# Chunks of alpha, k and q loaded in runs of one token, and the turned k sent by ScalarE's queue two slots apart

## The chip, the core and the metric

The kernel runs on one core of a Trainium2 chip. A core has TensorE (matmuls; the profile writes PE, and PEld for its weight loads), VectorE (DVE), ScalarE (ACT), GpSimd (POOL) and SyncE (SP), and 16 DMA engines. [...] The metric is the device time of one execution, in microseconds (us).

## What is computed

A gated linear recurrence over 768 tokens (batch 4, 8 heads, head dimension D = 48) feeds a two-layer network with a SiLU, over all 3072 tokens:

```python
def _attn_ref(q, k, v, alpha):
    state = np.zeros((B, H, D, D))
    for t in range(S):
        state = alpha[:, :, t, :, None] * state + np.einsum('bhd,bhe->bhde', k[:, :, t], v[:, :, t])
        y[:, :, t] = np.einsum('bhd,bhde->bhe', q[:, :, t], state)

def _moe_ref(x, w_in, w_out):          # x: 3072 x 384, d_ff: 2048
    h = x @ w_in
    g = h * (1.0 / (1.0 + np.exp(-h)))
    return g @ w_out
```

## The kernel before

**The recurrence.** The 768 tokens of a batch row are cut into 6 chunks of C = 128, so there are NT = 24 chunks n = 0..23, chunk index `ci = n // 4`, batch row `b = n % 4`. A chunk is worked in stages. `products(n)` brings alpha, then k, into the layout [two heads x 64 partitions, tokens], scans alpha (`u`, L734) and multiplies k by it into `kp`. `quotient(n)` does the same for q (scan L764, product L770). `scores(n)` multiplies kp and qp on TensorE; ScalarE copies the result out of PSUM (L818, L821) and GpSimd masks it (L825). `values(n)` multiplies by v, and `states(n)` adds k-transposed times v to the state of the batch row. For `states`, k is needed with tokens on the partitions, as tile `kn`.

**Early and late chunks.** Chunks 0..7 (`n < NA`, NA = 8) are transposed on TensorE. From chunk 8 on (the "late" chunks; 16 of them) three tiles `late["quads"]` hold alpha, k and q (`at`, `kt`, `qt` in the profile), one buffer each. VectorE transposes them in blocks of 32 x 32 by `turned` (L708), three times per chunk: `al<-at`, `turn<-kt`, `turn<-qt`. Right after each, `load(n + 1, name)` fills the tile for the next chunk. A DMA of `load` (L486) writes 32 partitions, 4 heads, 4 neighbouring tokens of 48 floats in one run (768 bytes). Four of them make one tile: each half of the heads is written twice, the second time 32 columns further left, so that the upper 32 partitions hold elements 32 to 47 in the columns where the lower hold 0 to 31. As partition b holds tokens 4b to 4b+3, the transpose has to write with a step of four elements to put the tokens in order.

**k for `states`.** `flip(n)` (late chunks with `ci < 5`, that is n = 8..19) transposes `kp` on VectorE (L780) into the one buffer `turn`, and SyncE at once writes that tile to a DRAM scratch `flips` (L782, 256 KB). In the next step `land(n)` reads it back with the blocks rearranged, in four DMAs of 64 KB (L790), into `kn`. The tile `turn` has one buffer, used in turn by the transposed k, the transposed q and the flip.

**The order.** The loop over steps (STEPS = 25) has four slots per step; after each slot `fill` emits pieces of the network's matmuls that have come due. For the late steps, with a lag of 1 for the stages that work on the chunk of the step before:

```python
stages = [[(land, 1), (scores, 1)], [(products, 0)], [(quotient, 0)],
          [(values, 1), (states, 1), (flip, 0)]]
```

TensorE's instructions are kept in the order in which this loop writes them. On the other engines the framework's scheduler may move an instruction past others, by its own estimates, except where `tc.keep_in_program_order` forbids it; what it decides is then fixed in the program. The loads of SyncE stand in one queue; each of its DMAs signals one of eight semaphores in rotation, and waits until the transfer that used the same semaphore before it has landed.

**The network.** Groups of 512 tokens go through `enter` (w_in) and `leave` (w_out), with block products in the manner of Strassen and Winograd. `enter` cycles through three PSUM banks `ps_m`: a product goes into a bank, ScalarE copies it out (L950), VectorE adds it to what is there (L958), and SiLU runs on ScalarE (L955; L923 in the plain form of the first groups, L863 is the copy of `values` into `xt`). `leave` uses two banks `ps_o` (copies L1054, L1073, L1078 on ScalarE, sums L1047 and L1056 on VectorE). `audit` reads the weights and alpha again to check their range (L681, L683, L697); its last tiles go through the quads once the chunks are done.

Of the kernel before, what the change touches and what calls it, by code (L numbers as in the profile page):

```python
# [8 lines left out]
F32 = mybir.dt.float32  # L9
I32 = mybir.dt.int32  # L10
# [345 lines left out]
def quotients(  # L356
# [19 lines left out]
    nc = tc.nc  # L376
    dve, act, gps = nc.vector, nc.scalar, nc.gpsimd

    late = {}
# [14 lines left out]
    B, H, S, D = q.shape  # L394
    C = 128
    NCH = S // C
    NP = H // 2
    HD = H * D
# [3 lines left out]
    NT = B * NCH  # L402
# [9 lines left out]
    def pool(name, bufs=1, space=None):  # L412
        kw = {} if space is None else {"space": space}
        return ctx.enter_context(tc.tile_pool(name=name, bufs=bufs, **kw))
# [10 lines left out]
    dram = pool("dram", 2, bass.MemoryType.DRAM)  # L425
# [29 lines left out]
    NA = 2 * GB  # L455
# [8 lines left out]
    ctxs = {}  # L464

    def load(n, names="akq"):
        if n == NT:
            return
        c = ctxs.setdefault(n, dict(zip(("ci", "b"), divmod(n, B))))
        b, rows = c["b"], slice(c["ci"] * C, c["ci"] * C + C)  # L470
        for name, src in (("a", alpha), ("k", k), ("q", q)):
            if name not in names:
                continue
            x = src[b, :, rows, :]
            if n < NA:
                c[name] = nat[name][n % NIN]
                nc.sync.dma_start(c[name][:, :, 0:D], x.transpose([1, 0, 2]))
                continue

            c[name] = late["quads"][name]
            for u in range(2):
                for i in range(2):
                    r = 64 * u + 32 * i
                    nc.sync.dma_start(  # L486
                        c[name][r : r + 32, 32 * (1 - i) :][:, 0 : 4 * NP * D].rearrange(
                            "p (g c) -> p g c", g=NP),
                        x[u::2].rearrange("h (b j) d -> b h (j d)", j=4))

    NV = 2
    vns = [fix.tile([128, H, 64], F32, name=f"vn{i}") for i in range(NV)]
# [3 lines left out]
    def load_v(n):  # L496
        c = ctxs.setdefault(n, dict(zip(("ci", "b"), divmod(n, B))))
        x = v[c["b"], :, c["ci"] * C : c["ci"] * C + C, :].transpose([1, 0, 2])
        t = c["v"] = vns[n % NV]
        if n < NA:  # L500
            nc.sync.dma_start(t[:, :, 0:D], x)
            return
        nc.sync.dma_start(t[:, 0 : H // 2, 0:D], x[:, 0 : H // 2])
        for e in range(2):
            nc.sync.dma_start(t[CH * e : CH * e + CH, H // 2 :, 0:D], x[CH - CH * e : C - CH * e, H // 2 :])
# [7 lines left out]
    def fetch():  # L513

        if wide and sources:
# [4 lines left out]
            coming.append(bits)  # L520

    load(0)
    load(1)
    for i in range(4):
        fetch()
# [47 lines left out]
    quads = w_in.rearrange("p k (q i c) -> p i k q c", i=4, c=128)  # L573
# [83 lines left out]
    def audit():  # L657


        flat = alpha.rearrange("b h s d -> (b h s d)").rearrange("(p c) -> p c", p=128)  # L660
        assert 2 * HD <= 32 + 4 * NP * D
        todo = [(flat[:, c : c + AW], AW, 0) for c in range(0, flat.shape[1], AW)]
        if wide:
            todo += [(moe_w_in[t * 128 : t * 128 + 128, c : c + 512], 512, 1)
                     for c in range(0, DF, 512) for t in range(NKT)]
            todo += [(moe_w_out[f * 128 : f * 128 + 128, :], HD, 1) for f in range(NFT)]
        alone = sum(2 * x[1] > 32 + 4 * NP * D or x[2] == 0 for x in todo)
        for kind in (0, 1):
            n = sum(x[2] == kind for x in todo)
            if n:  # L670
                seen.append([fix.tile([128, n], F32, name=f"seen{kind}{i}") for i in range(2)])
        at = [0, 0]
        landed = []

        def begin(src, n, kind):
            at = len(landed)
            t = late["look"].tile([128, 512, 2], I32, name="bits").rearrange("p n w -> p (n w)") if (
                at < alone) else late["quads"]["akq"[at % 3]].bitcast(I32)
            if kind == 0:
                landed.append(t[:, 0:n].bitcast(F32))  # L680
                nc.sync.dma_start(landed[-1], src)  # L681
            else:
                nc.sync.dma_start(t[:, 0 : 2 * n], src.bitcast(I32))  # L683
                landed.append(t[:, 0 : 2 * n].rearrange("p (n w) -> p n w", w=2)[:, :, 1])

        for i, (src, n, kind) in enumerate(todo):

            while len(landed) < min(i + (1 if i + 1 < alone else 3), len(todo)):
                begin(*todo[len(landed)])
            x = landed[i]  # L690
            yield
            i = at[kind]
            at[kind] += 1
            for which, op in ((0, ALU.max), (1, ALU.min)):
                if kind == 1 or which == 0:
                    tc.keep_in_program_order(
                        dve.tensor_reduce(seen[kind][which][:, i : i + 1], x, axis=AX, op=op,  # L697
                                          apply_absolute_value=True))
# [5 lines left out]
        return t[:, 1 : NP * W + 1].rearrange("p (j c) -> p j c", c=W)[:, :, 0:C]  # L704

    def turned(x, to):
        x = x[:, 32:].rearrange("p (g j d) -> p g j d", j=4, d=D)
        dve.transpose(to.rearrange("p g (b j) -> p g j b", j=4), x[:, :, :, 0:32])  # L708

    def products(n):  # L710

# [28 lines left out]
        if n >= NA:  # L740
            ps["k"] = late["turn"].tile([128, NP, C], F32, name="turn")
            turned(c["k"], ps["k"])
            load(n + 1, "k")
# [28 lines left out]
    def flip(n):  # L772

        c = ctxs[n]
        if n < NA or c["ci"] == NCH - 1:
            return
        t = late["turn"].tile([128, NP, C], F32, name="turn").rearrange("p c (j d) -> p c j d", j=NP)
        dve.transpose(t, c["kp"].rearrange("p j (c i) -> p c j i", i=32))  # L780
        c["flip"] = dram.tile([128, NP * C], F32, name="flips")
        nc.sync.dma_start(c["flip"], t.rearrange("p c j d -> p (c j d)"))  # L782

    def land(n):
        c = ctxs[n]
        if "flip" in c:
            c["kn"] = work.tile([128, NP, C], F32, name="kn")
            x = c.pop("flip").rearrange("(r d) (i x) -> i d r x", r=4, i=4)
            for i in range(4):
                nc.sync.dma_start(c["kn"][32 * i : 32 * i + 32], x[i])  # L790

    def scores(n):
        c = ctxs[n]
# [364 lines left out]
    def go_on():  # L1158
# [3 lines left out]
        done += 1  # L1162

    audits = audit()
    done, bridged = 0, 0
    STEPS = NT + 1
# [4 lines left out]
    def settle():  # L1171

        first.close()
        late.update(look=pool("look"), part=pool("part"), turn=pool("turn"),
                    xc=pool("xc").tile([128, len(SUMS_X), TB], F32, name="xc"),
                    wx=pool("wx").tile([128, 8, NQ, 128], F32, name="wx"))
        quads = pool("quads")
        late["p"] = pool("p").tile([128, NP * W + 1], F32, name="p")
        late["quads"] = {name: quads.tile([128, 32 + 4 * NP * D], F32, name=f"{name}t") for name in "akq"}
        for name, t in late["quads"].items():  # L1180
            gps.memset(t, 1.0 if name == "a" else 0.0)
        load(NA)
# [20 lines left out]
    for step in range(STEPS):  # L1203
        if step == 1:
            load(NIN)
        stages = [[(scores, 1)], [(products, 0)], [(values, 1)], [(states, 1)]]
        if step == 1:

            stages = stages[1::-1] + stages[2:]
        elif step >= NA:  # L1210
            stages = [[(land, 1), (scores, 1)], [(products, 0)], [(quotient, 0)],
                      [(values, 1), (states, 1), (flip, 0)]]
        for slot, group in enumerate(stages):
            for stage, lag in group:
                n = step - lag
                if not 0 <= n < NT:
                    continue
                stage(n)
                if stage is values:
                    bridged = n + 1  # L1220
                if stage is states and n + 1 + NIN < NA:
                    load(n + 1 + NIN)
                if stage is states and n + NV < NT:
                    load_v(n + NV)
            if step * SLOTS + slot == (NA + 1) * SLOTS - 1:
                x = decayed.rearrange("p (o i c) -> p o i c", o=2, c=C)
                for r, o in later:
                    gps.memset(x[r, o, :, 0:CH], 0.0)
            fill(step, slot)
            if step * SLOTS + slot >= NA * SLOTS - 1 and conv_done[1] == NFT and not late:  # L1230
                settle()
# [82 lines left out]
```

## Time and profile before

| what | us |
|---|---|
| median of 3 runs (556.2 to 557.51) | 556.21 |
| the profiled execution | 557.26 |
| its span, first to last instruction | 555.5 |
| TensorE busy in the span | 541.4 |
| VectorE busy | 445.4 |
| ScalarE busy | 208.5 |
| GpSimd busy | 76.1 |

The profile comes from one execution, 557.26 us long. Its span is 1.76 us shorter, and the median of the three runs lies 1.05 us below it. The granted TensorE clock was 0.999 of full speed. The page gives for each engine the busy time, for each group of instructions the mean duration and what ended the idle time before them, and for each group of DMAs the median from issue to landing. A line that begins with SPq is an instruction of SyncE's queue, with the time it took to issue. The view of waits lists for each engine whose work it waited for, with total, number and longest. The timeline lists instructions by start time; neighbours of one group are merged, with their number after the x. A float32 matmul is two records in the trace.

### The profile page before, as it was taken

What the parts mean: (1) busy time and instruction counts of PE and PEld (TensorE: products, weight loads), DVE (VectorE), ACT (ScalarE), POOL (GpSimd) and SP (SyncE); (2) the same over time, 40 slices, a digit from 0 to 9 for tenths busy, and PEclk for the clock granted to TensorE, in tenths of its full rate; (3) what the DMA queues carried; (4) which work ended last, traced back from release to release, by engine and by line L of the source; (5) the groups of instructions that cost most, each with busy time, mean ns of one, the idle gap of its engine ahead of it and who ended that gap; (6) DMA issues with size and microseconds to landing.
All of it is one profiled execution on the core that took longest, in us unless ns stands there. A gap on an engine that the chain in (4) does not pass through costs nothing. (4 is left out here: it accounts for less than half of the span.)

```text
span 555.5 us, 12640 instructions
## 1 busy us (share of the span) xinstructions
PE 541.4 (97%) x5026; PEld 489.7 (88%) x5026; DVE 445.4 (80%) x801; ACT 208.5 (38%) x466; POOL 76.1 (14%) x146
## 2 busy tenths in 40 slices
PE   6999999999999999999999999999999999999996
PEld 4788887998899999899999999988998999999996
DVE  5897788974999899997998986998884796945431
ACT  2556653223333253353353353344263342332100
POOL 3210000222210212021011021021121000001000
PEclk9999999999999999999999999999999999999999
DMA  9998971164454625355545654617642135500000
GB/s 215 246 249 210 232 195 33 47 161 116 117 136 125 159 63 138 86 145 149 139 112 139 193 139 120 191 27 183 170 137 91 54 91 169 172 11 22 10 24 30
DMA packets 99217, 70.09 MB, mean 126 GB/s; under 512 B 56272, under 2 KB 88656, under 8 KB 99152
## 3 DMA queue, kind: packets, MB, share of 16 engines
q1 hardware_dynamic: 97232, 65.30, 45.1%
q0 software_dynamic: 1920, 3.93, 2.0%
q8 instruction: 40, 0.66, 0.5%
q14 instruction: 25, 0.20, 0.1%
HBM read 61.34 MB, written 7.86 MB: 125 GB/s over the span
## 5 line engine op out<-in xcount | busy, mean ns | idle before, releaser
L388 PE MATMUL ps_o<-w_out,g 128*128 128x192 f32 x768 | 134.0, 328 | 0.5 <-DVE o L1056 0.5
L388 PEld LDWEIGHTS ps_o<-w_out,g 128*128 128x128 f32 x768 | 125.6, 190 | 3.5 <-DVE o L1056 1.0
L388 PE MATMUL ps_m<-xt,w_in 128*128 128x256 f32 x480 | 113.6, 383 | 1.5 <-ACT xt L863 1.1
L388 PEld LDWEIGHTS ps_m<-xt,w_in 128*128 128x128 f32 x480 | 89.1, 190 | 14.4 <-ACT xt L863 1.6
L388 PE MATMUL ps_o<-wt,g 128*128 128x192 f32 x576 | 99.7, 326 | 0.0
L388 PEld LDWEIGHTS ps_o<-wt,g 128*128 128x128 f32 x576 | 95.1, 190 | 1.6 <-issue 0.2
L388 PE MATMUL ps_m<-xc,w_in 128*128 128x256 f32 x288 | 70.7, 382 | 0.0
L388 PEld LDWEIGHTS ps_m<-xc,w_in 128*128 128x128 f32 x288 | 53.7, 190 | 7.0 <-DVE g L958 0.3
L1047 DVE TENSOR_TENSOR g<-g 128x512 f32<-128x512 f32 x72 | 50.1, 709 | 8.3 <-PE ps_o L388 8.3
L955 ACT ACTIVATE g<-g 128x1024 f32<-128x1024 f32 x32 | 33.1, 1056 | 61.2 <-DVE g L958 61.1
L1059 POOL DMA_DIRECT2D out_dram<-o x40 | 22.0, 551 | 219.5 <-DVE o L1056 113.7
L825 POOL TENSOR_SCALAR_AFFINE_SELECT g<-g 64x256 f32<-64x256 f32 x64 | 34.9, 546 | 124.4 <-ACT g L818 105.7
L388 PE MATMUL ps_m<-xc,wx 128*128 128x256 f32 x192 | 50.1, 383 | 1.0 <-DVE xc L586 1.0
L950 ACT COPY g<-ps_m 128x512 f32<-128x512 f32 x64 | 36.6, 588 | 37.0 <-PE ps_m L388 36.9
L388 PEld LDWEIGHTS ps_m<-xc,wx 128*128 128x128 f32 x192 | 35.2, 190 | 5.2 <-ACT u L1078 1.2
L958 DVE TENSOR_TENSOR g<-ps_m,g 128x512 f32<-128x512 f32 x56 | 37.1, 683 | 3.2 <-PE ps_m L388 2.7
L734 DVE TENSOR_TENSOR_SCAN u<-al,one 128x516 f32<-128x516 f32 x24 | 29.8, 1240 | 11.9 <-ACT al L731 11.6
L923 ACT ACTIVATE g<-ps_m 128x512 f32<-128x512 f32 x32 | 19.1, 597 | 41.7 <-PE ps_m L388 41.4
L950 ACT COPY part<-ps_m 128x512 f32<-128x512 f32 x32 | 18.9, 590 | 38.0 <-PE ps_m L388 24.0
L697 DVE TENSOR_REDUCE seen<-bits 128x1 f32<-128x512 int32 (+1 forms) x33 | 26.3, 823 | 5.7 <-DMA bits<-in_moe_w_in_dram 5.7
L764 DVE TENSOR_TENSOR_SCAN p<-al,inv 128x516 f32<-128x516 f32 x24 | 29.9, 1247 | 1.0 <-PE ps_a L388 0.3
L1056 DVE TENSOR_TENSOR o<-ps_o,u 128x192 f32<-128x192 f32 x24 | 8.5, 355 | 25.7 <-PE ps_o L388 22.8
(129 smaller groups left out, 648.5 us busy)
## 6 DMA issues: line engine op xcount, KB each, us to landing
bits<-in_moe_w_in_dram SPq DMA_DIRECT2D x24, 512.0 KB, 4.7
bits<-in_moe_w_out_dram SPq DMA_DIRECT2D x16, 384.0 KB, 3.9
at<-in_alpha_dram SPq DMA_DIRECT2D x64, 96.0 KB, 2.5
kt<-in_k_dram SPq DMA_DIRECT2D x64, 96.0 KB, 2.6
qt<-in_q_dram SPq DMA_DIRECT2D x64, 96.0 KB, 2.7
bits<-in_alpha_dram SPq DMA_DIRECT2D x9, 512.0 KB, 4.0
out_dram<-o POOLq DMA_DIRECT2D x40, 96.0 KB, 2.4
flips<-turn SPq DMA_DIRECT2D x12, 256.0 KB, 2.4
```

The source lines that it names most:

```text
L388: in_order(nc.tensor.matmul(*args, **kw))
L697: dve.tensor_reduce(seen[kind][which][:, i : i + 1], x, axis=AX, op=op, apply_absolute_value=True))
L734: dve.tensor_tensor_scan(u[:, end - 1 :: -1], sg[:, end:0:-1], one[:, end:0:-1], 0.0, ALU.mult, ALU.add)
L764: dve.tensor_tensor_scan(p[:, 0:end], sg[:, 0:end], iv[:, 0:end], 0.0, ALU.mult, ALU.add)
L825: gps.affine_select(x, x, pattern=[[0, NP], [1, CH]], compare_op=ALU.is_ge, fill=0.0, base=0, channel_multiplier=-1)
L923: act.activation(gts[grp, h, pair][:, i : i + 2, q % 2, :], ps, AF.Silu)
L950: act.copy(to, ps)
L955: act.activation(x, x, AF.Silu)
L958: dve.tensor_tensor(to, a, b, op)
L1047: dve.tensor_tensor(cells(grp, h, pair, *to), cells(grp, h, pair, *x), cells(grp, h, pair, *y), ALU.subtract)
L1056: dve.tensor_tensor(o, x, y, ALU.add)
L1059: (gps if grp < NG - 1 else nc.sync).dma_start(out[r : r + C, c * HO : (c + 1) * HO], o)
```

## The change

1. `load`, late chunks: instead of four DMAs per tile (32 partitions x 4 heads x 768 bytes) there are eight (32 partitions x 4 tokens x 192 bytes), one for each head. Partition b now holds tokens b, 32 + b, 64 + b and 96 + b of its head. Only the lower 32 partitions of each half are written by DMA.
2. A new stage `beside` fills the upper 32 partitions: for alpha, k and q, and for both halves, ScalarE copies elements 32 to 47 (32 partitions x 4 x 4 x 16) from the lower ones: six copies per chunk. It stands in slot 0 for the chunk of the step.
3. `turned` reads the tile without the offset of 32 and writes the tokens in order, without the step of four.
4. `flip` only transposes. A new stage `away`, in slot 0 of the next step, issues the write to `flips` on ScalarE's queue; `land` moves from slot 0 to slot 2 of that step and issues its four DMAs on ScalarE's queue. All five are kept in program order.
5. The quads are 768 instead of 800 columns wide; `audit` follows.

```diff
             c[name] = late["quads"][name]
+            for g in range(NP):
+                for u in range(2):
+                    nc.sync.dma_start(c[name][64 * u : 64 * u + 32, g],
+                                      x[2 * g + u].rearrange("(j b) d -> b j d", b=32))
+
+    def beside(n):
+
+        for name in "akq" if NA <= n < NT else "":
             for u in range(2):
-                for i in range(2):
-                    r = 64 * u + 32 * i
-                    nc.sync.dma_start(
-                        c[name][r : r + 32, 32 * (1 - i) :][:, 0 : 4 * NP * D].rearrange(
-                            "p (g c) -> p g c", g=NP),
-                        x[u::2].rearrange("h (b j) d -> b h (j d)", j=4))
+                r = slice(64 * u, 64 * u + 32)
+                act.copy(ctxs[n][name][64 * u + 32 : 64 * u + 64, :, :, 0 : D - 32],
+                         ctxs[n][name][r, :, :, 32:D])
...
     def turned(x, to):
-        x = x[:, 32:].rearrange("p (g j d) -> p g j d", j=4, d=D)
-        dve.transpose(to.rearrange("p g (b j) -> p g j b", j=4), x[:, :, :, 0:32])
+        dve.transpose(to.rearrange("p g (j b) -> p g j b", j=4), x[:, :, :, 0:32])
...
         dve.transpose(t, c["kp"].rearrange("p j (c i) -> p c j i", i=32))
-        c["flip"] = dram.tile([128, NP * C], F32, name="flips")
-        nc.sync.dma_start(c["flip"], t.rearrange("p c j d -> p (c j d)"))
+        c["flip"] = t
+
+    def away(n):
+        c = ctxs[n]
+        if "flip" in c:
+            t, c["flip"] = c["flip"], dram.tile([128, NP * C], F32, name="flips")
+            tc.keep_in_program_order(
+                act.dma_start(c["flip"], t.rearrange("p c j d -> p (c j d)")))
...
             for i in range(4):
-                nc.sync.dma_start(c["kn"][32 * i : 32 * i + 32], x[i])
+                tc.keep_in_program_order(
+                    act.dma_start(c["kn"][32 * i : 32 * i + 32], x[i]))
...
-        late["quads"] = {name: quads.tile([128, 32 + 4 * NP * D], F32, name=f"{name}t") for name in "akq"}
+        late["quads"] = {name: quads.tile([128, NP, 4, D], F32, name=f"{name}t") for name in "akq"}
...
         elif step >= NA:
-            stages = [[(land, 1), (scores, 1)], [(products, 0)], [(quotient, 0)],
+            stages = [[(away, 1), (beside, 0), (scores, 1)], [(products, 0)],
+                      [(land, 1), (quotient, 0)],
                       [(values, 1), (states, 1), (flip, 0)]]
```

More of the change, by code (lines that the diff above doesn't have):

```diff
@@ L660, in audit @@
         flat = alpha.rearrange("b h s d -> (b h s d)").rearrange("(p c) -> p c", p=128)
-        assert 2 * HD <= 32 + 4 * NP * D
+        assert 2 * HD <= 4 * NP * D
         todo = [(flat[:, c : c + AW], AW, 0) for c in range(0, flat.shape[1], AW)]
@@ L666, in audit @@
             todo += [(moe_w_out[f * 128 : f * 128 + 128, :], HD, 1) for f in range(NFT)]
-        alone = sum(2 * x[1] > 32 + 4 * NP * D or x[2] == 0 for x in todo)
+        alone = sum(2 * x[1] > 4 * NP * D or x[2] == 0 for x in todo)
         for kind in (0, 1):
@@ L677, in begin @@
             t = late["look"].tile([128, 512, 2], I32, name="bits").rearrange("p n w -> p (n w)") if (
-                at < alone) else late["quads"]["akq"[at % 3]].bitcast(I32)
+                at < alone) else late["quads"]["akq"[at % 3]].rearrange(
+                    "p g j d -> p (g j d)").bitcast(I32)
             if kind == 0:
```

## The prediction, made blind

> **What bounds the kernel now.** I read the page's busy shares first, then the stages by windows, then TensorE's waits, then the groups the change touches.
>
> ```profile
> PE 541.4 (97%) x5026; PEld 489.7 (88%) x5026; DVE 445.4 (80%) x801; ACT 208.5 (38%) x466; POOL 76.1 (14%) x146
> ```
>
> The windows below are the late chunks (first and second row) and what follows; columns are length, then busy us of PE, PEld, DVE, ACT, POOL with instruction counts, clock, DMA share, GB/s.
>
> ```profile
> core 0: us, PE busy (x) PEld busy (x) DVE busy (x) ACT busy (x) POOL busy (x), PEclk, DMA share, GB/s
> 100.00:190.00 90.00, 89.26 (x1062) 81.15 (x1061) 74.21 (x130) 25.90 (x73) 17.50 (x32) 1.00 0.47 123
> 190.00:358.00 168.00, 167.60 (x1708) 153.49 (x1710) 155.20 (x273) 68.54 (x161) 25.14 (x48) 1.00 0.49 132
> 358.00:551.00 193.00, 191.31 (x1382) 178.66 (x1371) 135.10 (x252) 63.34 (x129) 18.44 (x33) 1.00 0.32 89
> ```
>
> TensorE is busy 448.2 of 451 us from 100 on. VectorE is the second bound: 155.2 of 168 us, 92%, from 190 to 358. Its waits after 100:
>
> ```profile
> PE ps_m L388 <- DVE xc L586: 1.0, 1, 1.0
> PE ps_o L388 <- DVE o L1056: 0.5, 1, 0.5
> PE ps_a L388 <- DVE p L770: 0.5, 1, 0.5
> PE ps_m L388 <- DVE g L958: 0.4, 1, 0.4
> ```
>
> Those are TensorE's waits: nearly all on VectorE, and tiny. So a faster VectorE has at most 2.8 us to give, of which 0.5 (L1056, at 531) lies after the late chunks and some 0.3 elsewhere; about 2 us are within reach. Every new wait of TensorE, on the other hand, is paid in full.
>
> The groups concerned (busy, mean ns | idle before), and the transfers (median us to landing):
>
> ```profile
> L708 DVE STREAM_TRANSPOSE al<-at 128x512 f32<-128x512 f32 x16 | 18.2, 1137 | 1.6 <-DMA at<-in_alpha_dram 1.5
> L708 DVE STREAM_TRANSPOSE turn<-kt 128x512 f32<-128x512 f32 x16 | 18.1, 1133 | 0.0
> L708 DVE STREAM_TRANSPOSE turn<-qt 128x512 f32<-128x512 f32 x16 | 17.8, 1110 | 0.3
> L780 DVE STREAM_TRANSPOSE turn<-kp 128x512 f32<-128x512 f32 x12 | 8.5, 708 | 0.1
> L818 ACT COPY g<-ps_a 128x256 f32<-128x256 f32 x32 | 10.4, 376 | 10.0 <-PE ps_a L388 10.0
> ...
> kn<-flips SPq DMA_DIRECT2D x48, 64.0 KB, 2.8
> ```
>
> And from the timeline, what ScalarE does last before TensorE first uses `kn`, for chunk 8 and for chunk 15:
>
> ```profile
> 135.99 0.60 ACT L923 ACTIVATE g<-ps_m 128x512 f32<-128x512 f32 x1 [1.99 <-PE ps_m L388]
> 140.03 0.52 PE L388 MATMUL ps_a<-vn,kn 128*32 128x48 f32 x32
> ...
> 270.64 1.06 ACT L955 ACTIVATE g<-g 128x1024 f32<-128x1024 f32 x1 [6.06 <-DVE g L958]
> 274.00 0.52 PE L388 MATMUL ps_a<-vn,kn 128*32 128x48 f32 x32
> ```
>
> Before, SyncE issued the four `kn` reads of chunk 8 from 131.44 and those of chunk 15 from 259.1, some 8 and 14 us ahead of use.
>
> **What the Trainium skill says.** "SBUF — State Buffer", section "Door 1: The DMA port swizzle": accesses within one 16-byte line run at full bandwidth, each step to a new line pays. The old transpose writes with a step of four floats, 16 bytes; the trace agrees: 1110 to 1137 ns against 708 for L780, which writes in order. "DMA: Bandwidth & Descriptors", section "Anatomy of one DMA": some 2 us of each transfer are fixed, mostly the confirmation of the last write; here 2.4 (`flips`) and 2.8 (`kn`). Same page, "Issuing engines are not separate DMA queues": another issuing engine only saves issue time on the first. So sending k by ScalarE doesn't make it land sooner; no run yet shows a DMA issued by ScalarE.
>
> **The change part by part.**
>
> *Transposes.* 48 of them, 54.1 us together, should fall to 708 ns each: 34.0. VectorE loses 20.1 us, 1.26 per chunk. All of it lies beside TensorE; worth at most the 2 us above. I take 1.5.
>
> *Loads.* Per chunk 24 DMAs for 12. Four issue in 1.80 us (timeline, L486), 0.45 each: 10.8 us for 5.4. Both forms have 128 runs per DMA, so I keep 0.45. With v (0.39 + 1.26) and without `flips` and `kn` SyncE issues 12.5 us per chunk; chunks are 16 to 21 us apart (uses of `kn` at 140.0, 156.8, 173.0 … 337.3, 357.9). It fits, at three quarters full early on. Bytes halve; the DMA engines stand at 0.47 to 0.49 of their time. Cost 0, hidden under TensorE; if that cover goes, `beside` waits.
>
> *Copies.* 96 on ScalarE, 256 elements each. Nearest row L818 (same length, from PSUM): 376 ns; the skill's "ScalarE: Activation LUTs" ("What ACT_TABLE_LOAD costs") prices 186 + 0.833 x 256 = 399 ns. I take 376: 2.3 us per chunk, 36 in all. ScalarE had 38%; with the DMA issues it reaches about half. Queued behind a copy that waits for its load stand the evictions of `ps_m`. A bank is due again after two other products (1.03 each) and a piece of `leave` (2.76), 4.8 us, of which its copy takes 0.6: waits below 4 us cost nothing.
>
> *`away`.* One issue of 0.55 on ScalarE. The next k transpose needs `turn` free, so it waits for the landing, 2.4 us. In the built order of the changed kernel (dated by its neighbours among TensorE's instructions, whose own order is unchanged) the two stand 2.1 to 3.7 us apart: up to 0.3 us of VectorE per chunk, inside its saved 1.26.
>
> *`land`.* Here is the path. In that built order ScalarE reaches the four issues only after one eviction or SiLU, which has a time in the trace of before. From its end to the first use of `kn`, by chunk 8 to 19: 3.44, 3.45, 6.04, 8.63, 6.32, 0.99, 6.32, 2.30, 6.32, 2.80, 6.32, 3.38 us. Needed: three issues ahead of the last, at SyncE's median 0.424 for L790, and 2.8 to landing: 4.07; for chunk 8 two copies of 0.376 stand in between: 4.82. So chunks 10, 11, 12, 14, 16, 18 are in time, by 2 us and more. The others are late by 1.38 (8), 0.62 (9), 3.08 (13), 1.77 (15), 1.27 (17), 0.69 (19): 8.81 us, and `states` is next in TensorE's queue, with everything behind it. Chunks 13 to 19 hang on a SiLU that waits for VectorE (L958); if VectorE comes 1.26 us sooner, they lose 1.26, 1.26, 1.26, 0.69 and 4.34 remain. I take the middle, 6.6. Bounds for a ScalarE issue, which no row shows: L790's fastest on SyncE, 0.31, and 0.65, the mean of a queue with waits in it (2.67 for four at 304.3); for landing, 1.8 to 4.1, the extremes the trace gives for `flips` traffic. That makes 1.3 at best and 16 at worst.
>
> *Sum.* +6.6 - 1.5 = +5.1 on the profiled execution: 557.26 + 5.1 = 562.4, span 560.6. The median lies 1.05 below the profiled run: 561.3.
>
> **The rivals.**
> - *A, `kn` late in half the chunks*: 561.3, range 558 to 567. For it: the gaps above. Against: ScalarE issues may be quicker.
> - *B, VectorE's relief wins (the other side)*: ScalarE issues at 0.31 and `kn` lands at the 1.8 minimum, so 2.8 us suffice (3.5 for chunk 8), and VectorE's savings add up from chunk to chunk until L958 comes 1.8 us sooner. Then no chunk waits, TensorE's 2.1 us on VectorE between 116 and 380 go, and it ends at 556.2 - 2.1 = 554.1. Below 1.8 us of lead, chunk 13 takes the gain back. Against: the median landing of 2.8.
> - *C, both cancel*: about 556.5.
> - *D, three queues in a ring*: SyncE's semaphores wait for ScalarE's DMAs, ScalarE's copies for SyncE's loads, VectorE's transposes for the copies. When a load is over 4 us late, evictions stop TensorE too: 1 us in each of 16 chunks beyond A's cost, 577; half of that 569. For it: 75% full queue, copies standing 0.3 to 1 us ahead of their transpose in the first chunks' order. Against: SyncE's DMAs ran 4 us ahead of their place in the order before.
>
> **How the numbers follow.** A 0.54, B 0.11, C 0.15, D 0.20. 0.3% (1.7 us) is about what a measurement here can tell. Slower: A and D, 0.74; same: C, 0.15; faster: B, 0.11. Range 555.2 to 571: below it lies most of B, above it half of D. A's own range stands beside it.
>
> **What would show it.** TRANSPOSE rows of `at`, `kt`, `qt` near 708 ns, VectorE near 425 us; 96 new ACT copies near 0.38 us; `kn<-flips` issued by ACT near 0.42 us each; a wait "PE ps_a <- DMA kn<-flips" in chunks 8, 9, 13, 15, 17, 19, some 6 us together, and none in the other six. I am wrong if `kn` has no such wait (B or C), if issues on ScalarE take over 1 us, or if the lost time stands behind `ps_m`, `ps_o` or `vn` (D).

## The result, and the profile after

The changed kernel takes 565.03 us (median of 6 runs, 564.11 to 567.31) against 556.70 for the kernel before (6 runs): a ratio of 1.0153, 95% interval 1.0131 to 1.0174. That is 8.3 us slower. The profiled executions, 565.86 and 557.26 us, differ by 8.6 us.

The page's busy line of the changed kernel:

```profile
PE 541.5 (96%) x5026; PEld 489.3 (87%) x5026; DVE 426.9 (76%) x801; ACT 247.8 (44%) x562; POOL 72.1 (13%) x146
```

TensorE works as long as before. VectorE is relieved by 18.5 us, ScalarE carries 39.3 us more. The windows of the changed kernel, with the columns of the prediction's table (length, busy us of PE, PEld, DVE, ACT, POOL, clock, DMA share, GB/s):

```profile
100.00:190.00 90.00, 87.11 (x981) 78.59 (x983) 67.94 (x129) 38.34 (x104) 16.74 (x31) 1.00 0.39 81
190.00:358.00 168.00, 166.15 (x1714) 152.08 (x1707) 143.28 (x270) 88.19 (x212) 21.94 (x47) 1.00 0.45 105
358.00:551.00 193.00, 189.64 (x1402) 176.53 (x1401) 132.18 (x250) 70.43 (x144) 17.36 (x33) 0.99 0.29 83
```

TensorE's busy time in the three windows has fallen from 89.26, 167.60 and 191.31: it idles where the late chunks are. What for, says its list of waits after 100 us (total us, times, longest):

```profile
PE ps_a L388 <- DMA kn<-flips: 5.1, 5, 2.8
PE ps_a L388 <- DMA at<-in_alpha_dram: 2.0, 1, 2.0
```

The second line, too, is a matmul `vn,kn`, that of chunk 9; the profile names another releaser for it. Together these are 7.0 us at the first use of `kn`. In all, TensorE idles 8.1 us after 100 us, against 2.6 before: 5.5 us more. By chunk, predicted (the full list, before any relief from VectorE) and measured in the trace:

| chunk | 8 | 9 | 13 | 15 | 17 | 19 | 10, 11, 12, 14, 16, 18 |
|---|---|---|---|---|---|---|---|
| predicted late, us | 1.38 | 0.62 | 3.08 | 1.77 | 1.27 | 0.69 | 0 |
| measured idle, us | 0.43 | 1.96 | 0.16 | 0.77 | 0.92 | 2.79 | 0 |

These are the same six chunks, with a sum of 7.0 us where the list has 8.8 and the forecast took 6.6; but chunk by chunk the sizes are off.

The groups touched (busy, mean ns | idle before), and `kn` from the view of one tile (ns to issue, min/median/max):

```profile
L713 DVE STREAM_TRANSPOSE al<-at 128x512 f32<-128x512 f32 x16 | 11.3, 709 | 11.2 <-ACT at L493 6.9 <-DMA kt<-in_k_dram 4.1
...
L493 ACT COPY qt<-qt 32x256 f32<-32x256 f32 x32 | 12.9, 402 | 11.1 <-DMA qt<-in_q_dram 10.3
```

```profile
L802 ACTq DMA_DIRECT2D kn<-flips x48: 309/375/455, 135.8 to 361.3; - x48
```

The transposes take 704 to 709 ns. The copies take 402, a little above the 376 that were used, and near 399, the estimate that follows from the Trainium skill's price of an ACTIVATE ("ScalarE: Activation LUTs", "What ACT_TABLE_LOAD costs").

**What the waits don't hold.** 5.5 us are not 8.6. Behind the longest wait, the 2.79 us of chunk 19 that ends at 365.02, the granted clock is halved. Windows of the changed kernel there (columns as above):

```profile
365.00:366.00 1.00, 0.98 (x35) 0.94 (x36) 0.39 (x3) 0.95 (x3) 0.00 (x0) 1.00 0.33 57
366.00:369.00 3.00, 3.00 (x12) 3.00 (x11) 2.73 (x6) 0.61 (x2) 0.00 (x0) 0.53 0.44 77
369.00:371.00 2.00, 2.00 (x38) 1.69 (x37) 0.92 (x2) 0.34 (x2) 0.00 (x0) 0.86 0.35 53
```

For 3.4 us (366.16 to 369.58) TensorE is "busy" at half speed: it does the work of 1.7 us. In the kernel before, full speed is granted throughout between 18 us and the last matmul. Lastly, from the end of the last matmul to the end of the span it is 5.75 us instead of 4.75. So 5.5 + 1.7 + 1.0 = 8.2 of the 8.6 us are found, for this execution. Not every execution has the halved clock: 1.7 us would take 0.003 from the mean clock, and two of the six runs, 564.11 and 564.45 us, have a mean clock of 0.999. They are 7.4 us slower than before and more, so the loss does not need it.

### The profile page after: what moved, and what is told of

The parts are those of the page before. It is cut to its first block, busy times and chain, and to the rows that moved or that the text cites. A ratio compares the mean times of both kernels' runs of the same rounds, so it can differ in the third digit from the quotient of the medians.

```text
span 564.1 us, 13172 instructions
## 1 busy us (share of the span) xinstructions
PE 541.5 (96%) x5026; PEld 489.3 (87%) x5026; DVE 426.9 (76%) x801; ACT 247.8 (44%) x562; POOL 72.1 (13%) x146
## 5 line engine op out<-in xcount | busy, mean ns | idle before, releaser
L388 PE MATMUL ps_o<-w_out,g 128*128 128x192 f32 x768 | 135.9, 331 | 0.8 <-DVE o L1068 0.5
L388 PEld LDWEIGHTS ps_o<-w_out,g 128*128 128x128 f32 x768 | 127.3, 192 | 3.9 <-DVE o L1068 0.8
L1059 DVE TENSOR_TENSOR g<-g 128x512 f32<-128x512 f32 x72 | 48.2, 684 | 11.6 <-PE ps_o L388 11.3
L837 POOL TENSOR_SCALAR_AFFINE_SELECT g<-g 64x256 f32<-64x256 f32 x64 | 30.1, 471 | 136.7 <-ACT g L830 124.1
L739 DVE TENSOR_TENSOR_SCAN u<-al,one 128x516 f32<-128x516 f32 x24 | 29.5, 1230 | 10.7 <-ACT al L736 10.6
L388 PE MATMUL ps_a<-g,vn 128*32 128x128 f32 x768 | 27.9, 281 | 1.8 <-POOL g L825 1.7
L388 PEld LDWEIGHTS ps_a<-g,vn 128*32 128x32 f32 x768 | 20.4, 111 | 9.1 <-issue 6.5
```

The lines of the kernel that those rows point to most:

```text
L388: in_order(nc.tensor.matmul(*args, **kw))
L739: dve.tensor_tensor_scan(u[:, end - 1 :: -1], sg[:, end:0:-1], one[:, end:0:-1], 0.0, ALU.mult, ALU.add)
L837: gps.affine_select(x, x, pattern=[[0, NP], [1, CH]], compare_op=ALU.is_ge, fill=0.0, base=0, channel_multiplier=-1)
L1059: dve.tensor_tensor(cells(grp, h, pair, *to), cells(grp, h, pair, *x), cells(grp, h, pair, *y), ALU.subtract)
```

## The experiments

Each kernel was timed beside the kernel before on the same chip, which took 556.7 to 557.3 us there; ratios are to it. "Idle" is TensorE's idle time at the first use of `kn`, by chunk.

| run | loads of alpha, k, q | flips and kn | median us | ratio (95%) | idle at kn |
|---|---|---|---|---|---|
| changed kernel | new | ScalarE, slots 0 and 2 | 565.03 | 1.0153 (1.0131 to 1.0174) | 8, 9, 13, 15, 17, 19: 7.0 |
| e1_loads_alone | new | SyncE, as before | 565.99 | 1.0157 (1.0132 to 1.0181) | 8 to 11: 6.0 |
| e2_queue_alone | old | ScalarE, 0 and 2 | 565.70 | 1.0175 (1.0151 to 1.0199) | 13, 15, 17, 19: 7.0 |
| e3_land_slot1 | new | ScalarE, 0 and 1 | 556.88 | 1.0001 (0.9990 to 1.0011) | none |
| e4_slots_on_synce | new | SyncE, 0 and 2 | 570.97 | 1.0252 (1.0237 to 1.0267) | 8 to 11: 11.2 |
| e5_away_at_once | new | ScalarE, 3 and 2 | 563.90 | 1.0117 (1.0091 to 1.0143) | 8, 9, 13, 19: 6.8 |
| e6_split_loads | old, cut in two | SyncE, as before | 566.56 | 1.0179 (1.0166 to 1.0192) | 8 to 11: 5.7 |
| e7_old_loads_slot1 | old | ScalarE, 0 and 1 | 559.53 | 1.0046 (1.0033 to 1.0059) | none |
| e8_slot1_at_once | new | ScalarE, 3 and 1 | 557.53 | 1.0019 (1.0007 to 1.0031) | none |
| e9_gpsimd_queue | new | GpSimd, at once and 0 | 559.71 | 1.0049 (1.0029 to 1.0068) | none |

### The loads alone

The theory was that `kn`, reached too late by ScalarE, is the whole loss; the rival, that the loads and copies cost it. The changed kernel, with

```diff
-        c["flip"] = t
-
-    def away(n):
-        c = ctxs[n]
-        if "flip" in c:
-            t, c["flip"] = c["flip"], dram.tile([128, NP * C], F32, name="flips")
-            tc.keep_in_program_order(
-                act.dma_start(c["flip"], t.rearrange("p c j d -> p (c j d)")))
+        c["flip"] = dram.tile([128, NP * C], F32, name="flips")
+        nc.sync.dma_start(c["flip"], t.rearrange("p c j d -> p (c j d)"))
...
-                tc.keep_in_program_order(
-                    act.dma_start(c["kn"][32 * i : 32 * i + 32], x[i]))
+                nc.sync.dma_start(c["kn"][32 * i : 32 * i + 32], x[i])
...
-            stages = [[(away, 1), (beside, 0), (scores, 1)], [(products, 0)],
-                      [(land, 1), (quotient, 0)],
+            stages = [[(land, 1), (beside, 0), (scores, 1)], [(products, 0)], [(quotient, 0)],
```

> Loads in runs of one token, ScalarE copies and ordered transposes as in the changed kernel; flips and kn on SyncE, written and read back where they were before. Late-k theory (the lost time is TensorE waiting for kn that ScalarE issues too late): no TensorE wait on kn above 0.5 us in all, TensorE's waits on VectorE near zero, 1 to 2 us faster than before (555 to 556). Rival, the ring (twice as many loads in SyncE's queue, and copies that wait for them, cost the time): at least half of the loss stays, 560 to 565, with TensorE waiting for kn or at behind SyncE's queue, which now carries 29 issues per chunk. VectorE busy near 427 us in both.

Measured: 565.99 us, as slow as the changed kernel. The first theory's forecast (555 to 556) fails; the rival's, that at least half of the loss stays, holds (its 560 to 565 is passed by 1 us). `kn` is late, but in chunks 8 to 11 (3.44, 0.41, 0.99, 1.17 us), and ScalarE has no part in it. The timeline of SyncE's queue in this run shows why (start, us for the issues of the line):

```profile
119.46 3.72 SPq L485 DMA_DIRECT2D qt<-in_q_dram  x8
123.28 3.74 SPq L485 DMA_DIRECT2D at<-in_alpha_dram  x8
127.12 5.06 SPq L485 DMA_DIRECT2D kt<-in_k_dram  x8
132.28 3.70 SPq L485 DMA_DIRECT2D qt<-in_q_dram  x8
136.08 0.39 SPq L508 DMA_DIRECT2D vn<-in_v_dram  x1
...
137.93 0.55 SPq L787 DMA_DIRECT2D flips<-turn  x1
138.57 1.36 SPq L485 DMA_DIRECT2D at<-in_alpha_dram  x3
140.45 1.73 SPq L795 DMA_DIRECT2D kn<-flips  x4
```

There is no gap: when the late chunks begin, the loads of chunks 8 and 9 stand in the queue one behind the other, 24 each, at 0.46 us. Here SyncE reaches the reads of chunk 8 at 140.45, and TensorE wants `kn` at 140.5. In the kernel before it reached them 9 us sooner:

```profile
131.44 1.74 SPq L790 DMA_DIRECT2D kn<-flips  x4
```

From chunk 12 on, with more time per chunk, SyncE has caught up.

### Is it the number of issues?

The loads of e1 differ in number, in the length of their runs and in their layout. So the number was changed alone: the kernel before, with every late load cut in two.

```diff
-                    nc.sync.dma_start(
-                        c[name][r : r + 32, 32 * (1 - i) :][:, 0 : 4 * NP * D].rearrange(
-                            "p (g c) -> p g c", g=NP),
-                        x[u::2].rearrange("h (b j) d -> b h (j d)", j=4))
+                    y = x[u::2].rearrange("h (b j) d -> b h (j d)", j=4)
+                    for w in (slice(0, 2), slice(2, 4)):
+                        nc.sync.dma_start(
+                            c[name][r : r + 32, 32 * (1 - i) :][:, 0 : 4 * NP * D].rearrange(
+                                "p (g c) -> p g c", g=NP)[:, w], y[:, w])
```

> The kernel before, with every late load of alpha, k and q cut in two (two heads each): the same bytes, the same runs of 768 bytes and the same layout, but 24 issues per chunk instead of 12; no copies, the old transposes, SyncE's queue. Theory 'SyncE's issue time': the loads of chunks 8 and 9 stand in front of kn's reads, kn is late in chunks 8 to 11 as with the new loads on SyncE, 5 to 7 us of TensorE waits on kn, and 563 to 567. Rival, the short runs (192 bytes) or the copies held SyncE's queue there: no wait on kn above 1 us, 556 to 558. Issues of half the size may be cheaper (0.3 us instead of 0.45): then some 2 to 4 us of waits, 559 to 562.

Measured: 566.56 us. The same bytes, the same runs of 768 bytes, the same transposes as before, and 9.9 us slower. Waits of TensorE and SyncE's queue in this run:

```profile
PE ps_a L388 <- DMA kn<-flips: 5.7, 4, 2.1
```

```profile
125.34 4.92 SPq L488 DMA_DIRECT2D kt<-in_k_dram  x8
130.37 3.66 SPq L488 DMA_DIRECT2D qt<-in_q_dram  x8
...
138.32 1.73 SPq L791 DMA_DIRECT2D kn<-flips  x4
```

`kn` is late in chunks 8 to 11 again. A load of half the size costs SyncE the same 0.46 us. The theory "SyncE's issue time" holds: 12 more issues per chunk on the queue that also carries `kn` cost as much as the whole change does, and more.

### The queue and the slots alone

The kernel before, with only `away` in slot 0 and `land` in slot 2 on ScalarE's queue (the diff is the change's own for `flip`, `away`, `land` and `stages`, without `beside`).

> Loads and transposes as before, no copies; only the write of flips (slot 0) and the four reads of kn (slot 2) go by ScalarE's queue. Late-k theory: TensorE waits for kn in chunks 8, 9, 13, 15, 17, 19 again, 5 to 9 us together, and 6 to 10 us slower than before (563 to 567); chunk 9 may wait less, as the copies and the doubled loads that held its third issue are gone (0.3 to 1.0 instead of 2.0). Rival, the ring: with 12 loads per chunk and no copies there is no ring, so 557 to 559 and kn waits below 2 us.

Measured: 565.70 us. The time and the sum of the waits are as expected, the chunks only in part: `kn` is late in chunks 13, 15, 17 and 19 (2.08, 1.41, 0.70, 2.79 us), but in time in chunks 8 and 9:

```profile
PE ps_a L388 <- DMA kn<-flips: 7.0, 4, 2.8
PE ps_m L388 <- DVE g L965: 1.1, 2, 0.7
```

Two things follow. The waits of chunks 8 and 9 in the changed kernel (0.43 and 1.96) belong to the new loads and copies: without them ScalarE issues the four reads within 1.3 us there; with them it takes 2.4 and 3.5 us. Which of the two holds the reads was not tried apart. And each half of the change alone (e1, e2) loses as much as both: the losses don't add up. The queue takes `kn` out of the way of the doubled loads, and puts it behind ScalarE's work.

### One slot earlier

The changed kernel, with `land` in slot 1 and everything else left:

```diff
-            stages = [[(away, 1), (beside, 0), (scores, 1)], [(products, 0)],
-                      [(land, 1), (quotient, 0)],
+            stages = [[(away, 1), (beside, 0), (scores, 1)], [(land, 1), (products, 0)],
+                      [(quotient, 0)],
```

> The changed kernel with land one slot earlier (slot 1), still on ScalarE's queue. In the built order ScalarE reaches the fourth read 3.4 to 9.1 us ahead of use in every chunk. Late-k theory: the waits on kn fall from 7.0 us to below 1.5, 2 us of VectorE's waits stay gone, and the time is 555 to 558. Rival, the ring or ScalarE as an engine too full: ScalarE's load is the same and so is SyncE's, so at least 4 us of the loss stay, 561 to 565. A second rival, turn held by the flip: away stands where it stood, so a late flip still holds VectorE in chunk 19 (3.4 us there), and TensorE pays up to 2.8 us of it, 558 to 560.

Measured: 556.88 us, ratio 1.0001. No wait on `kn` is left:

```profile
PE ps_m L388 <- DVE xc L591: 1.0, 1, 1.0
PE ps_o L388 <- DVE o L1068: 0.5, 1, 0.5
```

ScalarE issues the first read 6.6 to 12.0 us before TensorE wants `kn`, in the changed kernel 2.2 to 9.1. ScalarE's and SyncE's loads are those of the changed kernel, so neither is too full: the slot makes the loss.

### The same slots on SyncE

```diff
             tc.keep_in_program_order(
-                act.dma_start(c["flip"], t.rearrange("p c j d -> p (c j d)")))
+                nc.sync.dma_start(c["flip"], t.rearrange("p c j d -> p (c j d)")))
...
                 tc.keep_in_program_order(
-                    act.dma_start(c["kn"][32 * i : 32 * i + 32], x[i]))
+                    nc.sync.dma_start(c["kn"][32 * i : 32 * i + 32], x[i]))
```

> The changed kernel with away in slot 0 and land in slot 2 as there, but issued by SyncE. Late-k theory, where only the time at which the issue is reached matters: SyncE has nothing but DMAs in its queue and ran some 4 us ahead of its place before, so kn lands in time in most chunks, waits of TensorE on kn 0 to 3 us, 555 to 559. Rival, the slots alone cost the time whatever the queue: 563 to 566 with the same six chunks late. Rival, the ring: SyncE's queue holds loads, write and reads, and kn stands behind loads that wait for VectorE to free kt and qt: waits on kn in other chunks than these six, 560 or more.

Measured: 570.97 us, the slowest of all. The first theory's forecast (555 to 559) fails. The third reading, 560 or more with `kn` behind loads, holds in the main: chunks 8 to 11 are late, of which 8 and 9 are among the six and 10 and 11 are not. SyncE's queue in this run, chunk 8:

```profile
136.78 0.55 SPq L793 DMA_DIRECT2D flips<-turn  x1
137.42 3.73 SPq L485 DMA_DIRECT2D at<-in_alpha_dram  x8
141.26 3.69 SPq L485 DMA_DIRECT2D kt<-in_k_dram  x8
145.00 1.84 SPq L802 DMA_DIRECT2D kn<-flips  x4
```

Two slots later means, on SyncE, behind 16 more loads: TensorE waits 8.71 us in chunk 8. That SyncE had run 4 us ahead of its place in the kernel before was no property of SyncE; with 24 loads per chunk it is gone.

### Was `turn` to blame in chunk 19?

In the changed kernel the k transpose of the next chunk waited for the write to `flips`, which landed 4.7 us after its issue:

```profile
349.10 0.71 DVE L713 STREAM_TRANSPOSE turn<-kt 128x512 f32<-128x512 f32 x1 [3.42 <-DMA flips<-turn]
```

The theory was that this made VectorE late, and with it the SiLU in front of the `kn` reads. So `away` was put right behind `flip`:

```diff
-            stages = [[(away, 1), (beside, 0), (scores, 1)], [(products, 0)],
+            stages = [[(beside, 0), (scores, 1)], [(products, 0)],
...
-                      [(values, 1), (states, 1), (flip, 0)]]
+                      [(values, 1), (states, 1), (flip, 0), (away, 0)]]
```

> The changed kernel with away right behind the flip (slot 3 of the same step) instead of slot 0 of the next, still on ScalarE's queue; land stays in slot 2. The write leaves some 3 us sooner, so turn is free sooner. Theory 'turn held by the late write' (chunk 19: flips landed after 4.7 us, the k transpose waited 3.4 us for turn, VectorE was late, and with it the SiLU ahead of the kn reads): chunk 19's wait falls from 2.8 us to about 0.7, the TensorE clock no longer halves behind it, the other five chunks stay late as they were; 3 to 4 us faster than the changed kernel, 561 to 562. Rival, the landing of kn beside the audit's transfers alone makes chunk 19 late: wait of 2 to 3 us stays, 564 to 566. Second rival, ScalarE now waits for VectorE's flip with evictions queued behind it: new TensorE waits on ps_m or ps_o, 565 or more.

Measured: 563.90 us. Its interval and the changed kernel's overlap, and the theory falls. The transpose no longer waits for `turn`, and the wait in chunk 19 is still 2.61 us. Timeline of this run:

```profile
345.90 0.70 DVE L713 STREAM_TRANSPOSE turn<-kt 128x512 f32<-128x512 f32 x1
...
360.05 1.06 ACT L967 ACTIVATE g<-g 128x1024 f32<-128x1024 f32 x1 [3.24 <-DVE g L970]
360.06 1.98 ACTq L802 DMA_DIRECT2D kn<-flips  x4
...
364.89 0.55 PE L388 MATMUL ps_a<-vn,kn 128*32 128x48 f32 x32 [2.61 <-DMA kn<-flips]
```

The SiLU starts where it started without this edit (360.00), 2.2 us before TensorE wants `kn`. The run bears on the clock too: 2.61 us of idle time, and this time full speed behind it. Two windows of it, 3.41 us long each; the last section says why they are taken there:

```profile
360.45:363.86 3.41, 1.83 (x57) 1.47 (x56) 2.88 (x6) 2.33 (x3) 0.54 (x1) 1.00 0.46 124
363.86:367.28 3.42, 2.39 (x44) 2.36 (x45) 3.19 (x7) 1.90 (x5) 0.00 (x0) 1.00 0.34 62
```

### What VectorE's relief and ScalarE's queue are worth

The old loads with ScalarE's queue and `land` in slot 1 (e2 with the edit of e3):

> Loads and transposes as before; only flips and kn on ScalarE's queue, with land in slot 1 instead of slot 2. Theory 'the slot alone makes the loss of the queue': no wait on kn, 556 to 558, like the kernel before. Rival, ScalarE's queue as such costs (its evictions held by five DMA issues per chunk): 559 or more. If VectorE's relief is worth something once kn is in time, this run is slower than the changed kernel with land in slot 1 (556.9) by 1 to 2 us; if not, equal within 0.5.

Measured: 559.53 us. No wait on `kn` is left, and yet the first forecast (556 to 558) fails and the rival's (559 or more) holds: with the old loads, ScalarE's queue and these slots cost 2.6 us (interval 1.8 to 3.3) even where `kn` is in time. The new loads with copies and ordered transposes give about as much back, since e3 stands at 1.0001; the intervals of the two ratios don't meet. TensorE's waits in this run:

```profile
PE ps_m L388 <- DVE xc L586: 1.3, 1, 1.3
PE ps_m L388 <- DVE g L965: 0.8, 2, 0.4
PE ps_o L388 <- DVE o L1063: 0.5, 1, 0.5
PE ps_m L388 <- ACT part L957: 0.4, 1, 0.4
```

TensorE idles 3.3 us after 100 us here and 1.9 us in e3; that is 1.4 of the 2.6 us. Against the kernel before, this profile has 0.7 us more of idle time and 1.2 us more from the last matmul to the end, but the end is as long in e3, which is not slower. So it is not shown that ScalarE's evictions, held by the DMA issues, make the 2.6 us, as the expectation had it.

### Two candidates for a better version

The changed kernel with both edits, `away` at once and `land` in slot 1:

> New loads, copies and transposes, ScalarE's queue, away right behind the flip and land in slot 1: the candidate for the best version. kn has 3.4 to 9 us of room in every chunk and turn is free sooner. Theory: no wait on kn; TensorE idle after 100 us below 2 us, as with land in slot 1 alone; 556 to 557, no measurable gain over the kernel before, since TensorE has under 3 us of idle time left to win. Rival, VectorE's freed time is worth its 2 us once nothing holds turn: 554 to 555.

Measured: 557.53 us, ratio 1.0019, and TensorE idles 2.2 us after 100 us. There is no gain, as expected, though both figures lie a little above the forecast (556 to 557, below 2 us). With under 3 us of idle time left to TensorE, freed time on VectorE has little to win.

The last candidate takes e1 and has GpSimd issue the write and the reads (`gps.dma_start` in both places):

> New loads, copies and ordered transposes; flips (at once) and kn (slot 0 of the next step, as before) issued by GpSimd, which is busy 14% of the time. In the built order the reads have 8 to 18 us of room. If the only thing that costs time is the point at which a busy engine reaches the reads, no wait on kn is left and ScalarE is spared five issues per chunk: 555 to 557, at best 1 to 2 us faster than before. Rival: GpSimd's own issues are dear and its masks of scores (which scores waits for) stand behind them: TensorE waits on vn or ps_a products behind masks, 558 or more.

Measured: 559.71 us. ScalarE is spared, the reads are issued 8.5 us and more ahead, `kn` is never waited for, and yet it is slower than before by 2.7 us (1.6 to 3.8). In its profile one wait of TensorE, in chunk 17, stands out. ScalarE's timeline ahead of it:

```profile
293.20 0.59 ACT L955 COPY g<-ps_m 128x512 f32<-128x512 f32 x1
300.81 0.40 ACT L493 COPY kt<-kt 32x256 f32<-32x256 f32 x1 [7.03 <-DMA kt<-in_k_dram]
301.24 0.48 ACT L868 COPY xt<-ps_a 128x384 f32<-128x384 f32 x1
```

A copy of `beside` waits 7.03 us for its load, the eviction of `xt` stands behind it, and TensorE waits 2.6 us for `xt`. This is a link of the prediction's ring (rival D), seen once. The clock is halved behind it for some 7 us. The profile is that of the slowest of the six runs (558.37 to 563.43 us), so it doesn't show what the median run loses. No version that was run beats the kernel before.

### The kernel before once more

> The kernel before, unchanged, profiled once more. All nine profiles of changed kernels have 5.7 to 6.8 us between the last matmul's end and the end of the span, the one profile of the kernel before has 4.75. If that is the run and not the kernel, 5.7 or more here; if the change lengthens the end (longer programs, other code positions), 4.7 to 4.9 again. TensorE idle after 100 us near 2.6 and no halved clock before the last matmul in both cases.

Measured: 557.17 us, 5.00 us from the last matmul to the end, 2.7 us of idle time after 100 us, no halved clock before the last matmul. So the end of all ten other kernels (5.74 us and more) is longer by 0.7 us and more than in both profiles of the kernel before. What in it is longer was not tried; e3 has it too and is no slower than before.

## Why the prediction was right, and where its sizes were not

The forecast was slower, 561.3 us in 555.2 to 571; it is slower, 565.03. The mechanism is the one named as the likeliest, `kn` late in six of the twelve chunks, the six that were named, and e3 shows it: with `land` one slot earlier the waits and the loss are gone. That the sum came so near, 7.0 us of waits for 6.6, is luck, as the part on `land` shows.

**Transposes.** 704 to 709 ns instead of 708, VectorE at 426.9 instead of "near 425". The worth, 1.5 us: TensorE's waits on VectorE at 143.8, 229.4 and 368.4 us in the trace before (1.8 us together) are gone after. But there TensorE comes later by its waits on `kn`. In e3, where it does not, the longest of them, 1.0 us on `xc`, is back, and the idle time after 100 us has fallen from 2.6 to 1.9 us only. Against the old loads on the same queue and slots, the new ones are worth 2.5 us, copies paid (e3 against e7, ratios 1.0001 and 1.0046).

**Loads, "cost 0".** Right for the changed kernel only in part, and for the wrong reason. Twelve more issues per chunk cost SyncE what was reckoned, 0.46 us each, but three quarters full was a mean: where the late chunks begin, two chunks' loads are issued without a gap, and anything behind them comes 9 us (e1) or 7 us (e6) late. In the changed kernel `kn` is no longer behind them, but the copies wait for them; that this makes the waits of chunks 8 and 9 is read from the timeline below and from e2, which has neither. The Trainium skill says of issuing engines ("DMA: Bandwidth & Descriptors", section "Issuing engines are not separate DMA queues") that another one only saves issue time on the first; e6 shows what that time can be worth: issues of 0.46 us alone cost 9.9 us.

**Copies, "cost 0".** 402 ns each; nothing on `ps_m`. What was missed: the reads of `kn` stand among them. In chunk 9 ScalarE waits for a load of `qt` inside the sequence. ScalarE's timeline in the changed kernel:

```profile
152.81 0.41 ACT L493 COPY qt<-qt 32x256 f32<-32x256 f32 x1 [2.47 <-DMA qt<-in_q_dram]
153.04 0.36 ACTq L802 DMA_DIRECT2D kn<-flips  x1
153.24 0.40 ACT L493 COPY qt<-qt 32x256 f32<-32x256 f32 x1
153.66 0.60 ACT L935 ACTIVATE g<-ps_m 128x512 f32<-128x512 f32 x1
153.77 3.11 ACTq L802 DMA_DIRECT2D kn<-flips  x3
```

The first issue then comes 3.81 us before TensorE wants `kn`, and the third of the four waits until 155.93, while loads of `at` are issued on SyncE from 153.50 on. That it waits for a semaphore (the counter by which an instruction waits for a transfer to land) that it shares with one of these loads is a reading of the trace, not tried. It cost 1.96 us where 0.62 had been reckoned.

**`land`, the mis-sized term.** Its sum was +6.6, and the waits are 7.0; three errors in it cancel, by luck. (Its bounds are not of one kind either: 1.3 lets half of VectorE's relief count, as 6.6 does, while 16 lets all of it count. Reckoned as 6.6 was, the worst is 18.)

- The start. The sum let ScalarE issue when its preceding SiLU has ended. It issues beside it. Timeline of the changed kernel, chunk 13:

```profile
229.87 1.06 ACT L967 ACTIVATE g<-g 128x1024 f32<-128x1024 f32 x1 [1.87 <-DVE g L970]
229.88 1.76 ACTq L802 DMA_DIRECT2D kn<-flips  x4
```

  So the lead is 1.06 us longer than reckoned. In e2, with VectorE's work as before, chunk 13 has 2.01 us from the first issue until TensorE wants `kn`: 0.99 + 1.06 = 2.05. In the changed kernel it has 3.48, 1.5 us more: hence 0.16 us of wait instead of 3.08. It may be VectorE's 1.26 us, which the prediction let come sooner or not, or TensorE's own 2.39 us of waits in chunks 8 and 9, which e2 lacks and which let VectorE catch up; these were not tried apart. In e5, with the short transposes and 2.86 us of such waits, the lead is only 2.24 us: there a scan (L739) stands ahead of the sums on VectorE.
- The landing. From the first issue to use 4.07 us were reckoned. Measured in chunks 13, 15, 17, 19: 3.64, 4.76, 5.02, 5.01. The last of the four reads is used 2.3 us after its issue in chunk 13, and 3.4 to 3.7 in the other three, for 2.8 reckoned. Reads of the audit run beside these; that they are the cause was not tried.
- Chunk 19. Before, the SiLU begins 4.4 us ahead of the use of `kn`; after, 2.2 us before TensorE wants it (2.1 in e2, 2.2 in e5). So not the transposes' length, as e2 has the old ones, and not `turn`, as e5 shows. VectorE's other work stands differently around that SiLU's sums in these kernels; which part delays it stays open. It makes 2.2 of the 2.79 us; with the SiLU where it was, the 5.01 us from issue to use would leave 0.6.

**What the sum lacked.** 5.5 us more idle time stand against 5.1 forecast, so the balance of waits was nearly met. The profiled execution took 3.5 us more than its forecast of 562.4. Of these, 2.7 are the halved clock (1.7) and the longer end (1.0), and no step had either.

**The rivals.** B failed as its premise did: issues at 0.375 us in the median, landing above 1.8. C's 556.5 is what e3 measures, but with `land` in another slot, and no wait on `kn` is made up for there: none is left. Of D's ring, a copy that waits for its load held TensorE up once in e9 and, if the timeline is read rightly, in chunk 9 here; not in every chunk.

## What to carry to other kernels

A transfer that a later matmul needs has to be dated on the queue it is put on, by the work that stands in front of it there: one slot of program order was worth 8 us here, and 12 more issues per chunk of 0.46 us each in front were worth as much. A queue's mean load hides its fullest stretch; count the issues back to back where a phase begins. Two parts of a change that each lose 1.6 to 1.8% alone need not lose 3% together (here 1.5%), so an edit that loses should be tried with its parts apart and its place moved before it is dropped.

## What the hardware showed that was not expected

**A wait of some 2.6 to 2.8 us can halve the clock for 3.4 us or more.** Behind 2.79 us (changed kernel), 2.79 (e2), 3.44 (e1) TensorE ran at 0.5 for 3.4 us; behind 2.58 (e9) for 7 us; around 8.71 (e4) for 10.2 us; behind 2.61 and 2.19 (e5), 2.08 (e2), 2.06 (e6) and 1.96 (changed kernel) not at all.

The traces say where the difference lies. Between two changes the granted clock stays for a whole multiple of 3.413 us: 126.29 us (37 times) in e1, 283.31 (83 times) in e9, 348.16 (102 times) in the changed kernel. So the changes lie on a grid of such windows that does not start with a wait. The windows of the grid that hold most of the wait, of the changed kernel, then of e9 with the next one; e5's are shown above:

```profile
362.75:366.16 3.41, 1.14 (x36) 1.11 (x37) 2.80 (x5) 3.31 (x7) 0.00 (x0) 1.00 0.33 76
...
298.25:301.66 3.41, 0.94 (x5) 0.36 (x3) 1.93 (x3) 0.82 (x2) 0.31 (x1) 1.00 0.57 125
301.66:305.07 3.41, 3.30 (x36) 3.17 (x37) 1.87 (x4) 2.65 (x10) 0.81 (x2) 0.50 0.52 124
```

The Trainium skill ("TensorE: Matmul & The Clock Gate", Part 1, "What's actually happening") has the clock fall to one half after an idle window of about 3.4 us, and calls the windows free-running. All three agree, but the window need not be idle throughout. Between 20 us and the last matmul, TensorE was idle for 2.27 (changed kernel), 2.47 (e9), 2.76 (e2), 2.94 (e1) and 3.11 us (e4) of the window ahead of each halving, and for at most 1.93 (e2) of any window that none followed. e5's 2.61 us are parted into 1.58 and 1.03. In the first 20 us one case doesn't fit: in the changed kernel, 1.73 us of idle time from 11.18 to 14.59 were followed by a halving. Nor is it shown why e9 stays at half for a second window, though TensorE idled for only 0.11 us of the first. All this is read off runs made for something else; none set the idle time.

**ScalarE issues a DMA while its compute instruction runs**, as in chunk 13 above: 0.375 us in the median for a 64 KB read, and the four reads begin within 1.3 us where nothing holds them.

**An issue costs SyncE much the same for a quarter of the bytes**: 0.44 us for 96 KB (before, four in 1.75), 0.46 for 48 KB (e6, eight in 3.66) and 0.46 for 24 KB (e1, eight in 3.72).
